# One list in place of ranks: the order of 2667 pieces of work in a sparse attention and SwiGLU kernel

## The chip, the cores and the metric

The kernel runs on one core of a Trainium2 chip. The metric is the device time of one execution in microseconds (us). Lower is better. The work is issued on five queues, each in order: TensorE (PE), VectorE (DVE), ScalarE (ACT), GpSimd (POOL), and SyncE (SP), which here only starts DMA transfers.

## The reference

Attention over 4 batches, 8 heads, 768 tokens of head size 64, with a block mask (blocks of 32 tokens: neighbours, first and last block, and 3 drawn blocks for each block row), then a SwiGLU feed-forward layer over all 3072 tokens.

```python
scores = scale * np.matmul(q, k.transpose(0, 1, 3, 2))
scores = np.where(mask, scores, -1000000000.0)
attn = np.exp(scores - max); attn = attn / (sum + 1e-09)
attn_out = np.matmul(attn, v)
x = attn_out, heads side by side            # 3072 x 512
g = x @ w_gate; val = x @ w_val             # 512 -> 1536
out = (g * sigmoid(g) * val) @ w_out        # 1536 -> 512
```

The weights arrive as 64-bit floats and are decoded on the chip.

## The kernel before

The tokens are cut into 9 chunks (`CHUNKS`): chunks 0, 1 and 2 have 256 tokens each and make up batch 0, chunks 3 to 8 have 384 tokens each. A chunk first goes through attention and then through the feed-forward layer. Chunks 0 and 1 are computed in f32, which needs only the decoded weights; later chunks use weights split into two f16 halves.

Nothing is issued where it is written. Each piece of work (a task) is handed to `add` with its engine, an estimated duration, the tasks that it needs, the ring buffers that it takes, and a rank. The tasks are numbered as they are added, 0 to 2666. `Plan.order` then plays a model of the five engines: whenever an engine is free, the ready task of the lowest rank is next on it. `SHIFT` moves the rank of groups of tasks. The order that comes out is the order of issue, and so the order in each engine's queue. Within a queue nothing overtakes: an instruction that waits holds all that stand behind it.

Names that the steps below touch:

- `load_k0` (L564, L574, L583, L581): three DMAs bring batch 0's keys as f32; PE turns six tiles (`kT`), ACT and DVE keep them (`kst`).
- `open_q0` (L1268): queries of a 128-token tile, two DMAs of 128 KB each. Chunk 0 has q0 and q1, chunk 1 q2 and q3, chunk 2 q4 and q5. Buffers: chunks 0 and 1 take ring `qs`; chunk 2 takes the ring `q`, of which there is one buffer.
- `load_v0` (L600, L609): batch 0's values in three parts of 512 KB, and four DMAs of 192 KB that spread the first and last block over the value ring.
- `pair0`: attention of two block rows of batch 0. Keys are gathered (`kring`, L1299, L1301: DVE for q0, POOL for the rest), scores (PE, L1341, L1357), `top` (DVE, L1363), `power` (ACT, L1372), `turn` (PE, L1380), `turned` (ACT or DVE, L1386), `values` (ACT or DVE, L1318), `product` (PE, L1401), `scaled` (DVE, L1409), `x_turn` (PE, L1418), a copy into `xall` (ACT, L1465).
- `norm_v0` (L398 on ACT, tile `vsq`): three squares of the values; their sum scales chunk 2 and later.
- `weights` (L453 loads, L431 to L433 decode on DVE): 12 pairs d0.0 to d0.11 for gate and value, 6 for the output. A pair takes two of four buffers of `stage`, so at most two pairs are on their way. `square_w` (L398 on ACT, tile `wsq`) and `norm_w1` follow.
- `ffn_in` (L1687 for chunks 0 and 1, L1693 later), `ffn_out` (L1756): the feed-forward matmuls, tiles `p` and `po`.
- `open_q` (L814): the norm of a later batch's queries, four DMAs of 128 KB into ring `q`; called g6 for batch 1.

In the kernel before, `behind=first_loads[-1]` chained the loads of `load_k0`, `load_v0` and `open_q0` one behind the other, so their order among themselves was fixed as they were added; weight loads came behind the seventh of them.

Of the kernel before, what the change touches and what calls it, by code (L numbers as in the profile page):

```python
# [18 lines left out]
BLK = 32  # L19
# [27 lines left out]
SHIFT = {  # L47
# [54 lines left out]
}  # L102


class Task:
    __slots__ = ("eng", "us", "emit", "need", "rank", "take", "dma", "left", "outs", "next", "ready", "end", "no", "key", "late", "many")


class Buf:


    def __init__(self, ring):
        self.ring, self.users, self.tile = ring, [], None

    def free_at(self):
        ends = [t.end for t in self.users]
        return None if None in ends else max(ends)


class Plan:  # L120


    def __init__(self):
        self.tasks, self.depth, self.given = [], {}, {}
        self.key = ""

# [3 lines left out]
    def add(self, eng, us, emit, need=(), rank=0.0, take=(), use=(), dma=None, behind=None, late=0.0, many=1):  # L130
# [14 lines left out]
        self.tasks.append(t)  # L145
        return t

    def may_take(self, t, now):

        at = now  # L150
        asked = {}
# [1703 lines left out]
```

## Time and profile before

| | |
|---|---|
| median of 3 runs | 797.4 us (796.4, 797.4, 800.65) |
| profiled execution | span 798.2 us; the page gives no other time for it |
| instructions | 21196 |
| PE busy | 762.4 us (96%) |
| DVE busy | 547.4 us (69%) |
| ACT busy | 504.5 us (63%) |
| POOL busy | 205.7 us (26%) |
| HBM read, written | 79.50 MB, 11.01 MB |

The span runs from the first to the last instruction. A busy PE is not PE at its peak: the ends of matmuls are modelled, and the clock granted to TensorE has two levels, 1.2 and 2.4 GHz; a mean of 0.67 in a stretch says that the engine ran a good part of it at the lower one. A wait names what came last before the waiting instruction began; "issue" is time in which nothing that the profile shows was waited for.

### The profile page before, as it was taken

What the parts mean: (1) busy time and instruction counts of PE and PEld (TensorE: products, weight loads), DVE (VectorE), ACT (ScalarE), POOL (GpSimd) and SP (SyncE); (2) the same over time, 40 slices, a digit from 0 to 9 for tenths busy, and PEclk for the clock granted to TensorE, in tenths of its full rate; (3) what the DMA queues carried; (4) which work ended last, traced back from release to release, by engine and by line L of the source; (5) the groups of instructions that cost most, each with busy time, mean ns of one, the idle gap of its engine ahead of it and who ended that gap; (6) DMA issues with size and microseconds to landing.
All of it is one profiled execution on the core that took longest, in us unless ns stands there. A gap on an engine that the chain in (4) does not pass through costs nothing.

```text
span 798.2 us, 21196 instructions
## 1 busy us (share of the span) xinstructions
PE 762.4 (96%) x8098; PEld 489.2 (61%) x8098; DVE 547.4 (69%) x1658; ACT 504.5 (63%) x1211; POOL 205.7 (26%) x257
## 2 busy tenths in 40 slices
PE   3789999999999999999999999999999999999998
PEld 2557778884587566645665566645665566555655
DVE  5676898998898787742799866753798767731220
ACT  2687767587688686763598856754487757641221
POOL 3553511322033223201223222401223233101210
PEclk9889999999999999999999999999999999999999
DMA  8963537647877979478769994947878974330001
GB/s 205 259 220 118 193 146 260 205 125 230 198 151 172 212 169 197 91 197 265 159 134 182 269 227 114 203 97 211 188 133 179 228 177 105 69 69 19 1 1 39
DMA packets 171430, 128.08 MB, mean 160 GB/s; under 512 B 115008, under 2 KB 136896, under 8 KB 171328
## 3 DMA queue, kind: packets, MB, share of 16 engines
q1 hardware_dynamic: 165696, 109.42, 56.6%
q0 software_dynamic: 5632, 17.31, 8.5%
q8 instruction: 63, 1.03, 0.5%
q14 instruction: 39, 0.32, 0.1%
HBM read 79.50 MB, written 11.01 MB: 113 GB/s over the span
## 4 chain that ended last, share of the span: by engine, by line
PE 63%; DVE 18%; DMA 8%; issue 4%; ACT 4%; SPq 1%; DVEq 1%; ACTq 0%
PE p L1693 29%; PE po L1756 18%; PE pv L1206 4%; PE p L1687 3%; DMA q<-in_q_dram 3%; PE qk L1137 3%; DVE pp L394 2%; DVE act L1702 1%; DVE act L1707 1%; DMA pts<-pp 1%; DVE w1t L394 1%; DVE e L1151 1%; DMA stage<-in_k_dram 1%; DVE kring L1114 1%; PE qk L1341 1%
## 5 line engine op out<-in xcount | busy, mean ns | idle before, releaser
L1693 PE MATMUL p<-xall,w1t 128*128 128x384 f16 (+1 forms) x2016 | 326.8, 319 | 0.0
L1693 PEld LDWEIGHTS <-w1t 128*128 128x128 f16 x2016 | 191.2, 98 | 115.5 <-issue 8.5
L1715 POOL TENSOR_TENSOR h<-act,h 128x384 f16<-128x384 f32 (+1 forms) x108 | 101.6, 941 | 372.5 <-ACT h L1712 372.1
L1756 PE MATMUL po<-w2all,h 128*128 128x512 f16 (+1 forms) x900 | 195.3, 371 | 0.3 <-DVE w2all L394 0.3
L1756 PEld LDWEIGHTS <-h 128*128 128x128 f16 x900 | 84.6, 98 | 93.7 <-issue 5.6
L1712 ACT CAST h<-act 128x384 f16<-128x384 f32 (+1 forms) x108 | 50.8, 471 | 82.5 <-DVE act L1707 82.2
L1124 POOL DMA_INDIRECT w2all<-vd,vidx x66 | 62.8, 951 | 150.2 <-PE pv L1206 126.7
L1702 DVE SCALAR_TENSOR_TENSOR act<-act,p 128x384 f32<-128x384 f32 (+1 forms) x108 | 54.2, 504 | 65.2 <-ACT act L1698 64.5
L1687 PE MATMUL p<-xall,w1t 128*128 128x256 f32 x384 | 88.8, 384 | 0.4 <-DVE act L1702 0.3
L1168 ACT ACTIVATE e<-e,nb,es 128x256 f32<-128x256 f32 x132 | 78.2, 593 | 2.2
L1687 PEld LDWEIGHTS p<-xall,w1t 128*128 128x128 f32 x384 | 71.4, 192 | 12.0 <-DVE w2all L394 1.4
L1698 ACT ACTIVATE act<-p,gsc 128x384 f32<-128x384 f32 (+1 forms) x84 | 47.0, 560 | 31.2 <-PE p L1693 30.6
L1707 DVE SCALAR_TENSOR_TENSOR act<-act,hs,p 128x384 f32<-128x384 f32 (+1 forms) x84 | 49.7, 591 | 21.8 <-PE p L1693 18.8
L1206 PEld LDWEIGHTS <-w2all 128*128 128x128 f16 x1584 | 55.1, 98 | 13.9 <-issue 3.8
L394 DVE SCALAR_TENSOR_TENSOR pp<-e,rr,pp 128x256 f16<-128x256 f32 x132 | 61.2, 510 | 1.3 <-ACT pp L391 1.0
L391 ACT ACTIVATE pp<-e,rr 128x256 f16<-128x256 f32 x132 | 58.1, 496 | 3.7 <-DVE rr L782 2.5
L1206 PE MATMUL pv<-pts,w2all 128*128 128x64 f16 x1584 | 57.0, 193 | 2.8 <-DMA pts<-pp 2.8
L1151 DVE CUSTOM_DVE_ANT_1 e<-qk,msk 128x256 f32<-128x256 f32 x132 | 50.0, 417 | 2.8 <-issue 2.4
L1593 ACT ACTIVATE ot<-po,oc 128x512 f32<-128x512 f32 (+1 forms) x25 | 16.7, 667 | 42.9 <-PE po L1756 42.7
L1114 DVE COPY kring<-kst 128x256 f16 x198 | 38.9, 251 | 5.6 <-PE qk L1137 5.3
L1232 DVE TENSOR_TENSOR xall<-pv,xall 64x256 f16<-64x256 f32 x66 | 27.7, 420 | 21.1 <-ACT xall L1227 18.7
L1137 PE MATMUL qk<-kring,qs 128*32 128x256 f16 x1056 | 35.7, 274 | 0.2 <-DVE mx L1151 0.2
(187 smaller groups left out, 899.4 us busy)
## 6 DMA issues: line engine op xcount, KB each, us to landing
stage<-in_w_dram SPq DMA_DIRECT2D x36, 512.0 KB
w2all<-vd SPq DMA_DIRECT2D x66, 192.0 KB
qs<-qraw SPq DMA_DIRECT2D x72, 128.0 KB
out_dram<-ot SPq DMA_DIRECT2D x19, 256.0 KB
qn<-in_q_dram SPq DMA_DIRECT2D x36, 128.0 KB
qraw<-in_q_dram SPq DMA_DIRECT2D x36, 128.0 KB
stage<-in_v_dram SPq DMA_DIRECT2D x9, 512.0 KB
vd<-stage SPq DMA_DIRECT2D x9, 512.0 KB
```

Of the source, the lines that this page charges most:

```text
L391: nc.scalar.activation(hi, src, AF.Copy, scale=scale)
L394: nc.vector.scalar_tensor_tensor(lo, src, scale, hi, op0=ALU.mult, op1=ALU.subtract)
L1124: nc.gpsimd.indirect_dma_start(vf[0:96, 1, :], None, bt.vd, bass.IndirectOffsetOnAxis(ap=vidx[0:96, qb : qb + 1], axis=0))
L1137: nc.tensor.matmul(stv[u * BLK : (u + 1) * BLK, g].rearrange("p s k -> p (s k)"), o.q[:, l, h // 2, h % 2, col : col + BLK], kg[:, h].rear ...
L1151: nc.vector.tensor_tensor_reduce(ev[:, g], stv[:, g], o.g.msk[:, qb, :].unsqueeze(2).broadcast_to([P, 8, BLK]), scale=1.0, scalar=-3.0e38, ...
L1168: nc.scalar.activation(ev[:, g], ev[:, g], AF.Exp, bias=nb_[:, g : g + 1], scale=o.g.es[:, 0:1], accum_out=c["rs"][:, g : g + 1],)
L1206: nc.tensor.matmul(pvv[:, j, n % 2], vg[:, cc, l, 2 * j : 2 * j + 2, :], pq[:, g, m, cc, u : u + 2, :], start=i == 0, stop=i == 5,)
L1687: nc.tensor.matmul(t[:, 0:tc_], w[:, i + 1, k_ * P : (k_ + 1) * P], x_k(k_), start=k_ == 0, stop=k_ == NKT - 1)
L1693: nc.tensor.matmul(t[:, 0:tc_], w_[:, f, m, k_, :], x_k(k_, l), start=i == 0, stop=i == 11)
L1702: nc.vector.scalar_tensor_tensor(a_, a_, 1.0, pg.tile[:, 0:tc_], op0=ALU.add, op1=ALU.mult)
L1715: nc.gpsimd.tensor_tensor(hv(f)[:, 1, :], act.tile[:, 0:tc_], hv(f)[:, 0, :], op=ALU.subtract)
L1756: nc.tensor.matmul(po.tile[:, cs], hv(f)[:, l, ts_], w2h[:, f, m, cs], start=f == 0 and i == 0, stop=f == NF - 1 and i == 2)
```

## The change

`SHIFT` is gone, and so are the model of the engines in `Plan.order`, `may_take` and `free_at`. `TURN` lists all 2667 task numbers; `Plan.order` walks it and only asserts that each task's needs and buffers are met. The tasks, what they issue and their needs are unchanged, except that the chain `first_loads` is gone: the loads of `load_k0` and `load_v0` have no predecessor any more, the second tile of each `open_q0` comes behind its first, and a weight pair's first load has no predecessor.

```diff
-SHIFT = {
-    "a0.0": 215.65, "a0.1": -2208.54, "a1.0": 2743.2, "a1.1": -905.98, "a2.0": -5449.96, "a2.1": 1137, "a3.0": -2069.74,
...
+TURN = [
+    7, 0, 18, 1, 2, 3, 37, 5, 8, 9, 19, 10, 20, 4, 6, 22, 12, 14, 15, 11, 13, 16, 17, 21, 42, 43, 44, 25, 83, 41,
+    39, 23, 63, 64, 65, 80, 57, 27, 26, 45, 46, 66, 67, 47, 24, 35, 49, 48, 53, 62, 40, 51, 60, 79, 81, 68, 70, 84,
...
     def order(self):
...
+        assert sorted(TURN) == list(range(len(self.tasks)))
         done = []
...
+        for n in TURN:
+            t = self.tasks[n]
+            assert not t.left, f"task {n} stands before one that it needs"
...
-        a = add("SP", 0.37, lambda: load(0), need, rank, take=raw, behind=first_loads[6], dma=1.7)
+        a = add("SP", 0.37, lambda: load(0), need, rank, take=raw, dma=1.7)
...
-            o.done = add("SP", 1.2, lambda sub=sub, si=si: load(sub, si), [], rank + 0.2 * sub, behind=first_loads[-1],
-                         take=[] if sub else [buf], use=[buf] if sub else [], dma=2.0, many=2)
-            first_loads.append(o.done)
+            o.done = opener = add("SP", 1.2, lambda sub=sub, si=si: load(sub, si), [], rank + 0.2 * sub, behind=opener,
+                                  take=[] if sub else [buf], use=[buf] if sub else [], dma=2.0, many=2)
```

With the tasks numbered as they are added, the list gives each queue its new order. The head of SP's queue (k.2 is the third part of the keys, v.0 the first part of the values, e the four spread loads, d0.0a and d0.0b the two loads of a weight pair):

```
place   before  after        place   before  after
0       table   k.2          10      d0.1a   e
1       k.0     table        11      q1      q2
2       k.1     k.0          12      v.1     v.1
3       k.2     k.1          13      v.2     d0.0a
4       q0      v.0          14      d0.1b   d0.0b
5       v.0     q0           15      d0.0a   d0.1a
6       e       e            16      d0.0b   d0.1b
7       e       e            17      q2      q3
8       e       q1           18      q3      g6, first 4 DMAs
9       e       e            19      q4      d0.2a
```

After that v.2 stands at place 23 (before 13), the loads of d0.4 at 24 and 25 (before 25 and 26), q4 at 26 (before 19), q5 at 33 (before 22); from place 54 to 62 the two orders agree.

On the other queues, counted in tasks: the values copies w0.0 and w0.1 on DVE move from places 12 to 14 to places 18, 20 and 22, behind the first four `top`. On ACT the three value squares leave places 8, 15 and 17 for places past 60, and the weight squares q1.0 leave places 28 and 29 for 39 and 36. The decode of d0.1 moves on DVE from 28 to 30 to 44, 45 and 48. On PE the first feed-forward piece moves from place 37 to 31, chunk 2's first scores stay at 53. In chunks 3 to 8 the 45 score pieces move on PE by between 3 places later and 15 earlier, 5.5 earlier in the mean; the 78 products by between 7 later and 9 earlier, 1.0 earlier in the mean. For one pair of chunk 6 (b6.1.0 and b6.1.1) scores move from 341 to 326, the first product from 349 to 343. The norms of later values and keys (v1, k1, v2, k2, v3, k3) come 2 to 11 PE places earlier. The last 38 PE pieces (from the second piece of chunk 8's feed-forward layer on) stand as before.

## Rows read from the trace of the kernel before

**Rows 1.** Windows: stretch, length; PE, PEld, DVE, ACT, POOL busy; clock, DMA share, GB/s
```profile
0.00:10.00 10.00, 2.31 (x11) 2.28 (x12) 4.23 (x25) 1.88 (x2) 2.62 (x9) 1.00 0.66 196
10.00:20.00 10.00, 5.14 (x82) 3.17 (x81) 7.31 (x24) 3.92 (x6) 3.92 (x4) 0.88 1.08 214
20.00:30.00 10.00, 7.25 (x146) 5.30 (x145) 5.29 (x15) 6.29 (x22) 3.08 (x13) 0.67 1.05 306
30.00:60.00 30.00, 23.43 (x632) 15.97 (x631) 21.41 (x47) 23.18 (x61) 19.41 (x37) 0.90 0.77 218
60.00:100.00 40.00, 37.53 (x599) 30.55 (x598) 30.90 (x73) 29.22 (x75) 17.09 (x26) 0.98 0.47 156
100.00:160.00 60.00, 59.56 (x573) 48.73 (x572) 56.98 (x114) 39.34 (x97) 13.06 (x12) 1.00 0.60 202
160.00:200.00 40.00, 37.31 (x174) 24.96 (x173) 34.49 (x84) 33.58 (x62) 10.03 (x10) 1.00 0.59 176
200.00:600.00 400.00, 394.86 (x4112) 243.12 (x4111) 290.97 (x983) 274.31 (x667) 96.26 (x105) 1.00 0.79 179
```

**Rows 2.** Waits of PE over the whole span: total us, times, longest us
```profile
PE qk L1341 <- DMA q<-in_q_dram: 3.1, 2, 2.6
PE pv L1206 <- DMA pts<-pp: 2.8, 3, 1.3
PE pt L1380 <- ACT e L1372: 2.6, 4, 1.2
...
PE nrm_v L388 <- ACT stage L398: 2.4, 2, 1.3
```

**Rows 3.** Chain of work, first 40 us: start us, us, what
```profile
3.46 9.84 DMA q<-in_q_dram
13.31 13.91 DMA q<-in_q_dram
```

**Rows 4.** Timeline of SP's queue: start us, us, what, count
```profile
2.72 1.60 SPq L1268 DMA_DIRECT2D q<-in_q_dram  x2
4.36 0.88 SPq L600 DMA_DIRECT2D w2all<-in_v_dram  x1
5.28 4.30 SPq L609 DMA_DIRECT2D w2all<-in_v_dram  x4
...
12.24 1.61 SPq L1268 DMA_DIRECT2D q<-in_q_dram  x2
...
55.43 0.81 SPq L453 DMA_DIRECT2D stage<-in_w_dram  x2
```

**Rows 5.** Timeline of PE: start us, us, what, in brackets the idle time before
```profile
13.34 0.39 PE L1341 MATMUL qk<-kst,q 64*32 64x96 f32 x14 [0.47 <-DMA q<-in_q_dram]
...
18.47 0.32 PE L1357 MATMUL qk<-dupm,ones_h 128*128 128x192 bf16 x1 [0.96 <-issue]
...
26.90 0.77 PE L1341 MATMUL qk<-kst,q 64*32 64x96 f32 x9 [2.61 <-DMA q<-in_q_dram]
```

**Rows 6.** Timeline of DVE, values copies, first top, decode of d0.1
```profile
17.24 2.89 DVE L1318 COPY w2all<-w2all 32x512 f32<-32x512 f32 x6 [1.28 <-issue]
...
20.79 1.28 DVE L1363 TENSOR_REDUCE mx<-qk 128x2 f32<-128x512 f32 x2
...
34.99 0.68 DVE L431 TENSOR_SCALAR w1t<-stage 128x1024 int32<-128x1024 int32 x1
...
36.97 1.23 DVE L433 SCALAR_TENSOR_TENSOR w1t<-stage,w1t 128x1024 int32<-128x1024 int32 x1
```

**Rows 7.** Timeline of ACT, one value square and one weight square
```profile
30.97 1.05 ACT L398 ACTIVATE vsq<-w2all 128x1024 bf16<-128x1024 f32 x1
...
43.86 1.06 ACT L398 ACTIVATE wsq<-w1t 128x1024 bf16<-128x1024 f32 x1 [0.47 <-DVE w1t L433]
```

**Rows 8.** Timeline of PE, first feed-forward piece, chunk 2's first scores
```profile
60.50 1.71 PE L1687 MATMUL p<-xall,w1t 128*128 128x256 f32 x4
...
68.80 0.40 PE L1341 MATMUL qk<-kst,q 64*32 64x96 f32 x16
```

More of the change, by code (lines that the diff above doesn't have):

```diff
@@ L44 @@
 LANES = 8
-SHIFT = {
[54 rows of a table removed]
-}
+TURN = [
[137 rows of a table added]
+]
 class Task:
@@ L113, in __init__ @@
         self.ring, self.users, self.tile = ring, [], None
-    def free_at(self):
-        ends = [t.end for t in self.users]
-        return None if None in ends else max(ends)
 class Plan:
@@ L134, in add @@
         t.key = self.key if rank > -50.0 else ""
-        t.rank = rank + SHIFT.get(t.key, 0.0)
+        t.rank = rank
         t.need = [x for x in need if x is not None]
@@ L146, in add @@
         return t
-    def may_take(self, t, now):
-        at = now
-        asked = {}
-        for b in t.take:
-            n = asked.get(b.ring, 0)
-            asked[b.ring] = n + 1
-            i = len(self.given[b.ring]) + n - self.depth[b.ring]
-            if i >= 0:
-                given = self.given[b.ring]
-                f = given[i].free_at() if i < len(given) else None
-                if f is None:
-                    return None
-                at = max(at, f + SEM_US)
-        return at
@@ L164, in order @@
-    def order(self):
-        free = {}
-        waiting = {}
-        for t in self.tasks:
-            free.setdefault(t.eng, 0.0)
-            waiting.setdefault(t.eng, [])
-            if not t.left:
-                waiting[t.eng].append(t)
-        queue = 2.0
-        lanes = [0.0] * LANES
-        done = []
-        now = 0.0
-        while len(done) < len(self.tasks):
-            later = []
-            moved = False
-            for eng, list_ in waiting.items():
-                if free[eng] > now:
-                    later.append(free[eng])
-                    continue
-                best = None
-                for t in list_:
-                    if t.ready > now:
-                        later.append(t.ready)
-                        continue
-                    if best is not None and (t.rank, t.no) > (best.rank, best.no):
-                        continue
-                    at = self.may_take(t, now)
-                    if at is None:
-                        continue
-                    if t.many:
-                        at = max(at, lanes[t.many - 1])
-                    if at > now:
-                        later.append(at)
-                        continue
-                    best = t
-                if best is None:
-                    continue
-                t = best
-                list_.remove(t)
-                for b in t.take:
-                    self.given[b.ring].append(b)
-                free[eng] = now + t.us
-                t.end = now + t.us + t.late
-                if t.dma is not None:
-                    queue = max(max(queue, now + min(0.4, t.us)) + t.dma, t.end)
-                    t.end = queue + DMA_US
-                    for _ in range(t.many):
-                        lanes.append(max(lanes.pop(0), t.end))
-                for x in t.outs + t.next:
-                    x.ready = max(x.ready, t.end + SEM_US if x in t.outs else free[eng])
-                    x.left -= 1
-                    if not x.left:
-                        waiting[x.eng].append(x)
-                t.ready = now
-                done.append(t)
-                moved = True
-                later.append(free[eng])
-            if not moved:
-                assert later, "the tasks wait for one another"
-                now = min(x for x in later if x > now)
@@ new lines, in order @@
+    def order(self):
+        assert sorted(TURN) == list(range(len(self.tasks)))
+        done = []
+        for n in TURN:
+            t = self.tasks[n]
+            assert not t.left, f"task {n} stands before one that it needs"
+            for b in t.take:
+                b.taken = True
+                i = len(self.given[b.ring]) - self.depth[b.ring]
+                assert i < 0 or None not in [u.end for u in self.given[b.ring][i].users], f"task {n} takes a buffer in use"
+                self.given[b.ring].append(b)
+            t.end = float(len(done))
+            for x in t.outs + t.next:
+                x.left -= 1
+            done.append(t)
@@ L301, in tile_block_sparse_attn_swiglu @@
     tab = const.tile([P, NB * 6], I32, name="tab")
-    first_loads = []
-    def first(load):
-        first_loads.append(load)
-        return load
     def load_tab():
@@ L369, in tile_block_sparse_attn_swiglu @@
     t_pre = add("DVE", 1.5, before, [], rank=-250.0)
-    t_tab = add("DVE", 0.75, tables, [first(add("SP", 0.4, load_tab, rank=-400.0, dma=0.4, late=1.2)), t_pre], rank=-200.0)
+    t_tab = add("DVE", 0.75, tables, [add("SP", 0.4, load_tab, rank=-400.0, dma=0.4, late=1.2), t_pre], rank=-200.0)
     t_rep = add("DVE", 2.0, repeats, [t_tab], rank=TAB)
@@ L565, in load_k0 @@
                 raw[:, 2 * i : 2 * i + 2, :], k[0, i * 256 : (i + 1) * 256, :].rearrange("(t p) n -> p t n", p=P)),
-                [], rank, behind=first_loads[-1], dma=1.7))
-            first(loads[-1])
+                [], rank, dma=1.7))
         for t in range(NTB):
@@ L599, in part @@
         def part(i, rank):
-            bt.v0_loads.append(first(add("SP", 0.45, lambda i=i: nc.sync.dma_start(
+            bt.v0_loads.append(add("SP", 0.45, lambda i=i: nc.sync.dma_start(
                 v0[:, 2 * i : 2 * i + 2, :], v[0, i * 256 : (i + 1) * 256, :].rearrange("(t p) n -> p t n", p=P)),
-                [], rank, behind=first_loads[-1], dma=2.0)))
+                [], rank, dma=2.0))
         bt.v0_part = part
@@ L608, in load_v0 @@
             for n, r0 in enumerate((0, S - BLK)):
-                e0_done.append(first(add("SP", 0.45, lambda m=m, sl=sl, n=n, r0=r0: nc.sync.dma_start(
+                e0_done.append(add("SP", 0.45, lambda m=m, sl=sl, n=n, r0=r0: nc.sync.dma_start(
                     w2all[sl, n + 2 * m : 2 * V0_RING : 4, :],
-                    v[0, r0 : r0 + BLK, :].unsqueeze(1).broadcast_to([BLK, V0_RING // 2, DM])), [], rank, behind=first_loads[-1], dma=0.8)))
+                    v[0, r0 : r0 + BLK, :].unsqueeze(1).broadcast_to([BLK, V0_RING // 2, DM])), [], rank, dma=0.8))
     def more_v0(rank):
@@ L1257, in open_q0 @@
         o = Tile_q()
-        view = {}
+        view, opener = {}, None
         def load(sub, si):
```

188 rows, old and new, of tables (SHIFT, TURN) are left out of this document.

## The prediction

> **What bounds the kernel now.** I read the page's engine shares first: PE is busy for 762.4 of 798.2 us, so what an order can win is at most the 35.8 us in which PE is idle, and what its clock loses. The second view, the busy times by stretch, shows where that is [rows 1]. PE is idle for 7.7 us in the first ten, 4.9 in the next ten, 2.8 from 20 to 30, 6.6 from 30 to 60, 2.5 from 60 to 100, 0.4 from 100 to 160, 2.7 from 160 to 200, and 5.1 over the 400 us after that; what is left, 2 to 3 us, lies after 600, in the tail. So the kernel is bound by PE from about 60 us on, and by a mixture before. The reader should also see there that the clock was granted at 0.88, 0.67 and 0.90 of full speed from 10 to 60 us: busy time times the missing share is 5.14 x 0.12 + 7.25 x 0.33 + 23.43 x 0.10 = 5.4 us of PE work lost. And DVE is busy for 57.0 of 60 us from 100 to 160: there it is nearly as tight as PE.
>
> The third view, PE's waits, names causes: query loads 3.1 us, transposed probabilities in later chunks 2.8, the exponentials of batch 0 2.6, norms of values 2.4 [rows 2]. The fourth, the chain of waits in the first 40 us, consists of two query loads, 9.8 and 13.9 us long [rows 3]. The fifth, the queues' own timelines, says what each of these stood behind [rows 4 to 7].
>
> **The change part by part.** No instruction is added or removed, so every term is idle time or clock. Against the profiled execution, 798.2 us; the median of the runs is 797.4, and I take off 0.8 at the end.
>
> *Start and first queries.* The keys are loaded first as before, another part ahead; three parts and the table are the same bytes, so I count nothing, though after the last part PE has three tiles to turn instead of two. But q0 now stands behind the values' first part. Before, q0 was issued at 2.72, before the values' 0.88 us of issue [rows 4], and landed at 13.31 [rows 3]. Issued 0.9 later it lands at 14.2 at best. At worst it waits until both it and the values are in: the values copies on DVE begin at 17.24 [rows 6]. I take the middle, 15.7.
>
> The scores of the first pair started at 13.34 and the first `top` at 20.79 [rows 5, 6]. Between lie matmuls, which I estimate at 3.2 us (PE was busy for 5.14 us from 10 to 20, which holds the end of the turned keys too [rows 1]), and several waits, one of them 0.96 us of "issue" [rows 5] that I can't assign. With q0 at 15.7, 3.2 us of work and half a microsecond of such waits, `top` starts at 19.5, since no 2.89 us of values copies stand ahead of it on DVE any more [rows 6]. Gain 1.3. Bounds: 3.6 gained with q0 at 14.2 and no wait, 1.5 lost with q0 at 17.2 and all of the waits.
>
> The Trainium skill bears on this step ("DMA: Bandwidth & Descriptors", Queues, rings and completion order): each engine takes the descriptors of a ring in ring order. [...]
>
> *Second queries.* q1 was issued at 12.24, after all four spread loads (4.30 us of issue) and a weight load, and landed at 27.22 [rows 3, 4]; PE stood for 2.61 us until 26.90 [rows 5]. Now only two of the spread loads stand before it. Its issue follows from the issue times [rows 4]: 2.72, when table and keys are issued, + 0.88 values + 1.60 q0 + 2.15 for two spread loads = 7.35. With q0's 9.8 to 10.6 us from issue to landing it is there at about 17.9, with q1's own 15.0 at 22.3. PE was free for these scores at 26.90 - 2.61 = 24.3 and now is at 24.3 - 1.3 = 23.0, so the whole 2.61 us goes. Bounds: 0 (landing as late as before) and 2.61. What is late next is `kring` on POOL, which from 60 us backwards is the least loaded engine [rows 1].
>
> *What leaves the heads of ACT and DVE.* Three value squares of 1.05 us and two weight squares of 1.06 leave ACT's early queue [rows 7]: 5.3 us that stood between exponentials. The decode of d0.1, from 34.99 to 38.20, leaves DVE's [rows 6]: 3.2 us ahead of a `top`. PE's idle time from 30 to 60 us is 6.6 [rows 1], of which 2.6 are waits for exponentials [rows 2]. These pieces don't vanish; they are done later, where ACT has room (39 of 60 us busy from 100 to 160) but DVE has little (57.0 of 60). So I take a bit under half, 3.0. Bounds: 0 (all of it comes back) and 6.6.
>
> *Clock.* From 20 to 30 us 2.4 of the 5.4 us are lost, in the stretch with q1's stall. PE was idle there for 2.61 us before 26.90 [rows 5]. Without it I give back half, 1.2. Bounds 0 and 4.
>
> *Values' third part, q4, q5, g6.* v.2 comes ten places later on SP. Its first reader is then a value square past place 60 on ACT, so nothing waits unless the loads of d0.2 and d0.3 ahead of it hang on slow decodes. q4 goes from place 19 to 26, behind g6's first loads, and both need the single `q` buffer. Cost nothing if q4 lands before chunk 2's scores, which started at 68.80 [rows 8]; the place before it (d0.4's second load) was reached at 55.43 [rows 4]. This is the second rival below.
>
> *Later chunks.* Idle PE time from 160 to 600 us is 7.8 [rows 1], of which 2.8 are waits for transposed probabilities [rows 2]. Scores come 5.5 places earlier in the mean and products 1.0, so a product has 4 to 5 PE pieces more between it and its scores: that should shorten those waits. Against it, six norms come 2 to 11 places earlier and may stand longer for their squares (2.4 us before, for values). I take 0. Bounds: 2.8 gained, and 4 lost. The tail is the same 38 pieces: 0.
>
> Sum: 1.3 + 2.6 + 3.0 + 1.2 = 8.1; 798.2 - 8.1 - 0.8 = **789.3 us**. All good bounds together, 3.6 + 2.6 + 6.6 + 4 + 2.8 = 19.6, give 777.8; all bad ones, -1.5 - 4 = -5.5, give 802.9.
>
> **The rivals.**
>
> *The gain is given back (no change).* Early attention ends sooner, but the feed-forward layer of chunks 0 and 1 needs decoded weights, and DVE, which decodes them, is at 57.0 of 60 us from 100 to 160 [rows 1]. If the deferred 3.2 us of d0.1 and the rest of DVE's queue don't move forward into its idle time (22 us idle before 60, 9 from 60 to 100 [rows 1]), PE waits there for what it saved. For it: that tightness. Against it: the idle DVE time is just where the change puts attention earlier. Then only the 1.2 us of clock and a little remain: about 796.
>
> *Chunk 2's queries come too late (slower).* q4 waits for the `q` buffer until the square of g6's first load is done, 47 places down ACT's queue, and SP holds d0.6, d0.5, d0.7 and q5 behind it. If q4 is issued only at 55.4 + 0.8 = 56.2, where the place before it was done [rows 4], and takes the 15.0 us that q1 took, it lands at 71.2. PE, 8 us ahead, is at these scores at 60.7 and stands for 10.5 with everything behind it; the weights held back on SP cost as much again as one decode, 3.2. That gives 798.2 - 8.1 + 10.5 + 3.2 - 0.8 = 803.0. The point from which it decides is a landing of q4 later than about 61. For it: both orders of buffers and the late place. Against it: DMA engines are only 0.47 busy from 60 to 100 against 1.05 at the time of q1 [rows 1], so the landing should be much quicker.
>
> *The early stage fills completely (faster than forecast).* PE gets attention pieces without a break from 16 us on, the clock stays up, the whole of 6.6 and 4 come, and the later waits go: near 780. For it: DVE was idle for 22 of the first 60 us. Against it: products still need gathers on POOL and copies on ACT, 23.2 of 30 us busy from 30 to 60 [rows 1].
>
> **How the numbers follow.** Forecast (784 to 793) 0.56; given back (793.5 to 798) 0.17; q4 late 0.10; filled (776 to 784) 0.17. A difference of 0.5%, 4.0 us, is about what a measurement of this kernel can tell from no change. Faster than 793.4 takes the forecast and the filled case, 0.73; slower than 801.4 takes most of the late case, 0.08, and 0.02 for waits in the later chunks, 0.10; the rest is 0.17. The range is 778 to 798: below it lies little of the filled case, above it the late case and a tail of the given-back one. The forecast's own range is 784 to 793.
>
> **What would show each step.** In the new profile q0 should land at 14 to 17 us and q1 before 23, with no wait of PE for queries over 1 us. The first `top` should begin before 20. Value and weight squares should lie behind the exponentials of chunks 0 and 1, the first feed-forward matmul on PE should begin before 55 instead of at 60.50 [rows 8], and PE's idle time from 10 to 60 should fall from 14.2 to about 7. PE's waits for `pts` should not exceed 2.8 us, for norms not 6. Wrong would be: a wait of several us at chunk 2's scores on `q`, new idle PE time from 60 to 160 with DVE's decode as releaser, or waits spread over chunks 3 to 8.

## The result, and the profile after

The changed kernel takes 805.9 us, the kernel before 800.6 (medians of 13 runs each, side by side). The ratio, which leaves out one run of the kernel before that took 883.5 us, is 1.0077 [1.0052, 1.0102]: slower by 0.5 to 1.0%, where 789.3 us and a gain of 1% were forecast, and outside the range of 778 to 798. The profiled execution has a span of 805.2 us against 798.2, so 7.0 us are to be found.

The windows of the kernel after, in the same stretches and columns as [rows 1]:

```profile
0.00:10.00 10.00, 2.27 (x10) 1.90 (x11) 2.82 (x17) 1.31 (x2) 0.62 (x7) 1.00 0.60 202
10.00:20.00 10.00, 6.37 (x80) 4.41 (x78) 6.32 (x30) 2.27 (x4) 5.69 (x6) 0.85 1.12 209
20.00:30.00 10.00, 8.05 (x251) 6.02 (x246) 6.55 (x14) 6.76 (x23) 4.30 (x15) 0.81 1.05 312
30.00:60.00 30.00, 21.89 (x565) 16.35 (x547) 17.78 (x35) 18.70 (x55) 16.38 (x31) 0.89 0.59 145
60.00:100.00 40.00, 34.80 (x583) 27.49 (x581) 33.34 (x80) 33.34 (x79) 18.92 (x26) 0.96 0.61 193
100.00:160.00 60.00, 58.21 (x566) 47.88 (x565) 55.81 (x101) 38.20 (x94) 13.81 (x15) 1.00 0.64 211
160.00:200.00 40.00, 37.43 (x174) 25.49 (x174) 34.25 (x89) 34.39 (x65) 10.28 (x11) 1.00 0.59 162
200.00:600.00 400.00, 393.05 (x4157) 243.55 (x4156) 301.58 (x1018) 281.07 (x687) 94.74 (x103) 1.00 0.79 180
```

PE is idle for 3.6 us from 10 to 20 (4.9 before) and 2.0 from 20 to 30 (2.8), as hoped. Then it turns: 8.1 from 30 to 60 (6.6), 5.2 from 60 to 100 (2.5), 1.8 from 100 to 160 (0.4), 7.0 from 200 to 600 (5.1). From 10 to 60 us it sums to 13.7, where 14.2 were to become about 7. The columns after PEld say more: DVE does 33.5 us of work in the first 60 us (2.82 + 6.32 + 6.55 + 17.78), where it did 38.2, and ACT 29.0 against 35.3. That work is still to be done.

PE's waits, the lines that answer to [rows 2] and the new ones (total us, times, longest):

```profile
PE qk L1352 <- issue: 10.4, 7, 5.5
PE pv L1412 <- DMA w2all<-in_v_dram,vidx: 2.7, 1, 2.7
PE qk L1149 <- DVE mx L1163: 2.6, 3, 1.5
PE qk L1352 <- POOL kring L1312: 1.6, 1, 1.6
PE p L1704 <- DVE act L1713: 1.3, 1, 1.3
```

The wait for query loads (3.1 us) is gone from the list. In its place stands "issue", 10.4 us at the scores of batch 0. From the timeline of PE, the scores of q0 (two, then the other fourteen), the longest such wait, and the first feed-forward piece (start, us, what, in brackets the idle time before):

```profile
13.38 0.39 PE L1352 MATMUL qk<-kst,q 64*32 64x96 f32 x2
13.98 0.39 PE L1352 MATMUL qk<-kst,q 64*32 64x96 f32 x14 [0.21 <-issue]
...
36.03 0.79 PE L1352 MATMUL qk<-kring,q 64*32 64x160 f32 x15 [5.49 <-issue]
...
53.94 1.24 PE L1698 MATMUL p<-xall,w1t 128*128 128x256 f32 x5
```

The first feed-forward piece comes at 53.9 instead of 60.5 [rows 8], but six PE pieces fewer stand ahead of it (place 31 instead of 37), so this is not a lead of 6.6 us. To see what was won and where it went, compare starts at places of PE's queue that hold the same piece in both orders, with the same set of pieces before it. Place 60 is a feed-forward piece of chunk 0, place 74 one of chunk 1, place 154 the first of chunk 2, place 209 the second one of chunk 3. Of the kernel before:

```profile
86.84 1.89 PE L1687 MATMUL p<-xall,w1t 128*128 128x256 f32 x8
...
104.11 1.99 PE L1687 MATMUL p<-xall,w1t 128*128 128x256 f32 x8 [0.30 <-DVE act L1702]
...
215.23 0.94 PE L1693 MATMUL p<-xall,w1t 128*128 128x256 f16 x7
...
284.85 1.47 PE L1693 MATMUL p<-xall,w1t 128*128 128x384 f16 x8
```

And of the kernel after (the piece of place 209 lies inside the last group and starts at 290.5):

```profile
84.29 1.97 PE L1698 MATMUL p<-xall,w1t 128*128 128x256 f32 x8
...
104.42 1.89 PE L1698 MATMUL p<-xall,w1t 128*128 128x256 f32 x8
...
216.99 1.26 PE L1704 MATMUL p<-xall,w1t 128*128 128x256 f16 x10
...
289.50 2.11 PE L1704 MATMUL p<-xall,w1t 128*128 128x384 f16 x12
```

So PE is 2.5 us ahead at place 60, 0.3 behind at place 74, 1.8 behind at place 154, 5.6 behind at place 209 (69.7 us between the last two before, 73.5 after), and 6.7 at the last matmul (794.7 and 801.4). Nearly all of the loss lies ahead of place 209. Each of these is one execution, and executions differ: with the same order up to place 154 as the kernel before, e2, e6 and e10 come to it at 212.8 to 213.2 instead of 215.2. The time from place 154 to 209 repeats better: 69.6 to 70.5 us in the five kernels of this document that keep the order before in this stretch (before, e4, e6, e12, e14), 72.6 to 73.5 in the eleven with the new order on both sides of place 154 and all of its work (after, e3, e5, e7 to e9, e11, e13, e15 to e17). Between the two places, from the windows, first before, then after:

```profile
215.20:284.90 69.70, 68.13 (x949) 51.36 (x946) 58.46 (x238) 54.72 (x155) 20.64 (x25) 1.00 0.78 174
```

```profile
217.00:290.50 73.50, 69.00 (x946) 51.91 (x945) 65.76 (x242) 59.27 (x163) 20.72 (x25) 1.00 0.84 176
```

DVE has 65.8 us of work there instead of 58.5, and PE is idle for 4.5 us instead of 1.6. The groups of instructions on DVE in those stretches show which (count, total us, mean ns), before and after:

```profile
L394 DVE SCALAR_TENSOR_TENSOR w1t<-w1t,wsc 128x512 f16<-128x512 f32 x1 | 0.7, 744 | 0.0
```

```profile
L407 DVE SCALAR_TENSOR_TENSOR w1t<-w1t,wsc 128x512 f16<-128x512 f32 x7 | 5.2, 745 | 0.0
```

These are low halves of the split of the gate and value weights into f16. The new list puts seven of them behind place 154, between the `top` pieces of chunk 3 (DVE places 284 to 341, chunk 3's first `top` at 265). In the order before all 24 stand ahead of chunk 3's first `top`; one of them was still done after 215.2.

### The profile page after: what moved, and what is told of

It reads as the page before. It is cut to its first block, busy times and chain, and to the rows that moved or that the text cites. A ratio compares the mean times of both kernels' runs of the same rounds, so it can differ in the third digit from the quotient of the medians.

```text
span 805.2 us, 21103 instructions
## 1 busy us (share of the span) xinstructions
PE 761.7 (95%) x8098; PEld 490.9 (61%) x8098; DVE 553.8 (69%) x1658; ACT 503.8 (63%) x1211; POOL 205.3 (26%) x257
## 4 chain that ended last, share of the span: by engine, by line
PE 67%; DVE 13%; issue 6%; DMA 6%; ACT 5%; POOL 1%; SPq 1%; DVEq 1%; POOLq 0%; ACTq 0%
PE p L1704 31%; PE po L1767 22%; PE pv L1218 4%; PE qk L1149 3%; DMA stage<-in_w_dram 2%; PE qk L1352 2%; PE p L1698 1%; PE qkf L934 1%; DVE kring L1126 1%; DVE pp L407 1%; DMA w2all<-in_v_dram,vidx 1%; DVE act L1718 1%; PE pvf L1003 1%; DVE act L1713 1%; DVE e L1163 1%
## 5 line engine op out<-in xcount | busy, mean ns | idle before, releaser
L1726 POOL TENSOR_TENSOR h<-act,h 128x384 f16<-128x384 f32 (+1 forms) x108 | 97.1, 904 | 408.7 <-ACT h L1723 376.4
L1767 PE MATMUL po<-w2all,h 128*128 128x512 f16 (+1 forms) x900 | 191.4, 371 | 1.4 <-DVE act L1713 0.8
L1767 PEld LDWEIGHTS <-h 128*128 128x128 f16 x900 | 86.4, 98 | 95.7 <-issue 3.2
L407 DVE SCALAR_TENSOR_TENSOR pp<-e,rr,pp 128x256 f16<-128x256 f32 x132 | 63.1, 522 | 7.0 <-ACT pp L404 4.8
L1218 PEld LDWEIGHTS <-w2all 128*128 128x128 f16 x1584 | 52.6, 98 | 11.0 <-issue 3.5
L1604 ACT ACTIVATE ot<-po,oc 128x512 f32<-128x512 f32 (+1 forms) x25 | 16.6, 666 | 37.3 <-PE po L1767 32.2
```

The costliest lines, as they stand in the source:

```text
L407: nc.vector.scalar_tensor_tensor(lo, src, scale, hi, op0=ALU.mult, op1=ALU.subtract)
L1218: nc.tensor.matmul(pvv[:, j, n % 2], vg[:, cc, l, 2 * j : 2 * j + 2, :], pq[:, g, m, cc, u : u + 2, :], start=i == 0, stop=i == 5,)
L1726: nc.gpsimd.tensor_tensor(hv(f)[:, 1, :], act.tile[:, 0:tc_], hv(f)[:, 0, :], op=ALU.subtract)
L1767: nc.tensor.matmul(po.tile[:, cs], hv(f)[:, l, ts_], w2h[:, f, m, cs], start=f == 0 and i == 0, stop=f == NF - 1 and i == 2)
```

## The experiments

Two theories came out of the traces. F: PE's "issue" waits are instruction fetch held up by data. During each of the two long ones a 16 KB transfer of the queue that section 3 of the page calls instruction is on its way, and they begin after PE's instructions 449 and 705, 256 apart (weight loads and all else in its queue counted). G: work for DVE was put off and comes back where DVE is nearly full.

**Which part costs: the early order, the late order, or the form?**

```diff
 e1: -TURN = new order
     +TURN = new order up to PE place 154, then the order before
 e2: -TURN = new order
     +TURN = order before up to PE place 154, then the new order
 e6: -TURN = new order
     +TURN = order before (as a list, without the chain of first loads)
```

> The new order for everything up to the 154th PE piece (about the first 195 us), then the rest in the order of before. PE's idle time up to 200 us was 27.5 us before and 31.0 after, beyond it 8.3 and 12.5. Theory S (two separate losses): this kernel keeps the early 3.5 us and gives up the late 4.2, so about 801 to 802 us of span, a ratio to before of 1.004. Rival L (the late loss follows from the early one, because what is late at 200 us stays late): ratio near 1.008. Rival M (all of it is the late part): 1.000.

Measured 1.0134 [1.0093, 1.0174], more than any of the three theories said. The cut itself makes a wait, so this run does not price the early order. It moves the last low halves ahead of chunk 3's first `top`, nine in a row, each of which waits for its high half on ACT; PE stands for 7.3 us, and takes 80.5 us from place 154 to 209. PE's wait, and one of the nine:

```profile
PE qk L1157 <- DVE mx L1171: 7.3, 1, 7.3
```

```profile
208.20 0.75 DVE L415 SCALAR_TENSOR_TENSOR w1t<-w1t,wsc 128x512 f16<-128x512 f32 x1 [0.72 <-ACT w1t L412]
```

> The order of before up to the 154th PE piece, then the rest in the new order. Theory S: the late 4.2 us alone, ratio 1.005, PE idle before 200 us as before (27.5 us), beyond it near 12. Rival L: 1.000, the late order costs nothing once the early part is in time. Rival M: 1.008.

Measured 0.9971 [0.9945, 0.9998]. The late order as a whole does not cost. In this run all 24 low halves stand ahead of chunk 3's first `top`, as before, and the rest is the new order from place 154 on; place 209 comes 71.5 us later:

```profile
212.80:284.28 71.48, 68.50 (x948) 51.78 (x945) 62.66 (x246) 56.30 (x159) 22.42 (x25) 1.00 0.81 169
```

> The order of before, written as a list in the new kernel, with the chain of first loads gone. If the order alone counts: ratio 1.000 within 0.3%, the same waits as before. Rival: the form or the chain costs something, ratio off 1 by more than 0.5%.

Measured 1.0001 [0.9976, 1.0025]. The list and the missing chain cost nothing. With e2, the loss is in the order up to about place 154 on PE and in what it puts off past that place.

**Theory F: early waits**

```diff
 e3: -raw[.., n*512 : (n+1)*512] as four pieces of 512 bytes a row (open_q)
     +raw[sl, n*512 : (n+1)*512] from 512 neighbours, one piece of 2 KB a row
 e4:  order before, SP:  -q3, q4, ...   +q3, g6 first 4 DMAs, ..., q4
 e5:  the new kernel again, on another chip
 e7:  new order, SP:  -d0.0a d0.0b d0.1a d0.1b q3 g6
                      +q3, 16 bytes written once the 2nd pair's rr is there, d0.0a d0.0b d0.1a d0.1b g6
 e8:  new order, POOL: -key copies of b2.0.0, its two value gathers
                       +its two value gathers, key copies
 e9:  e3 + e7 + e8, and the next pair's gathers early too
```

> The new order unchanged; the queries that are loaded for a batch's norm alone (open_q) come in pieces of 2 KB instead of 512 bytes, the same bytes in another arrangement, which leaves the sum of squares as it is. Theory F (PE waits for its instructions, whose 16 KB fetch stands among the 512-byte pieces of the norm load on the DMA engines): the wait of 5.5 us at 30.5 us, in the middle of a score piece, falls below 2 us and the span by 3 to 5 us, to about 801. Rival W (the fetch takes its time whatever the other transfers are, or the wait has another cause): the wait stays between 4.5 and 6.5 us and the time at the new kernel's, ratio 1.008.

Measured 1.0034 [1.0004, 1.0064]. The wait that was to fall below 2 us is 3.84 (and the one ahead of it 2.65). e18 has 3.84 there too, with the short pieces: no support for the piece size.

> The order of before, with one thing of the new one: the first norm load of batch 1's queries (four DMAs in 512-byte pieces) goes to place 19 of SP's queue, its square to ACT's place 51, and chunk 2's first queries come behind. Theory F: a wait of PE on issue alone, 2 to 5 us long, appears between 28 and 42 us, and the time is 2 to 4 us longer, ratio 1.003 to 1.005. Rival W: no new wait of that kind, ratio 1.000, or a loss only at chunk 2's first scores, at about 69 us.

Measured 0.9999 [0.9971, 1.0027]. A wait appears where F puts it, behind instruction 705, and the time does not move. e14, which does not load the norm early, has one of 2.0 us at the same instruction, so the norm load is not shown to be its cause:

```profile
30.75 0.38 PE L1360 MATMUL qk<-kst,q 64*32 64x96 f32 x3 [2.41 <-issue]
```

> The new kernel itself, on the chip that runs the next three. All theories: ratio to before 1.005 to 1.010. Theory F (PE waits for its instructions): PE stands on issue exactly behind its 449th and its 705th instruction, 256 apart, each time for a 16 KB fetch that runs late, 6 to 7.5 us together, and chunk 2's feed-forward layer begins at 208 to 217 us as in the two profiles of this early order so far. Rival N (what the first profile showed was that one run's): the waits stand elsewhere or are under 3 us together.

Measured 1.0059 [1.0036, 1.0083], with waits of 1.2 and 6.0 us at the same two instructions.

> The new order, but the first four weight loads (2 MB) and the norm load stand behind q3 and behind a 16-byte transfer that waits for the second pair's reciprocals (34 us in the last profile, sooner if PE isn't held up); the first decode pass comes three DVE places later. Theory F: with those 2.5 MB out of the way the fetches that PE needs behind its 449th and 705th instruction run 1 to 3 us after they are asked for instead of 5 to 6; the two waits fall from 6.5 to under 3 us together, the first feed-forward piece begins 3 to 5 us sooner than in the new order on this chip, and the time falls by 2 to 5 us unless the later weights cost it: ratio 1.001 to 1.005. Rival W (a fetch takes 6 us whatever else is on its way): the waits stay at 6 to 7 us, the weights come later, ratio 1.008 to 1.012.

Measured 1.0051 [1.0024, 1.0077]. The timeline of PE, at the same two instructions:

```profile
27.50 0.49 PE L1364 MATMUL qk<-kring,q 64*32 64x160 f32 x12 [1.28 <-issue]
...
31.25 0.50 PE L1364 MATMUL qk<-kring,q 64*32 64x160 f32 x15 [1.10 <-issue]
```

The two waits fall from 7.2 (e5, same chip) to 2.4 us, which supports F on what they are. The time falls by 0.1%, within the error, but the price of the waits is not isolated by that: 2 MB of weights come later here, and new waits of the kind appear, of 1.1 and 1.5 us behind instructions 961 and 1217. All of PE's "issue" waits from 20 to 217 us come to 9.5 us in e5 and still to 8.5 in e7.

> The new order, with the two gathers of chunk 2's first pair (POOL) ahead of that pair's key copies, as they stood before, instead of behind four more key copies. Theory G (PE's wait of 2.7 us for gathered values, with 1.6 us for POOL's key copies in front of it, is a loss of its own): the 2.7 us go and the time falls by 2 to 3 us against the new order on this chip, ratio 1.004 to 1.006. Rival D (behind it PE would have waited for decoded weights or chunk 2's chain anyway): the wait goes, others take its place between 85 and 160 us, ratio as the new order's, 1.007 to 1.009.

Measured 1.0038 [1.0017, 1.0058]. The wait of 2.5 us near 91 is gone, and the next pair's gathers make one of 3.2 us:

```profile
104.42 1.08 PE L1420 MATMUL pv<-w2all,pts 128*32 128x64 f32 x32 [3.23 <-DMA w2all<-in_v_dram,vidx]
```

> The new order with three repairs at once: the first four weight loads and the norm load of batch 1 held behind q3 and a 16-byte marker transfer, the norm loads in pieces of 2 KB (other elements of the queries are squared, the sum is the same), and the gathers of the next two pairs ahead of the key copies on POOL. Alone they gave about 0.1%, 0.3 to 0.4% and 0.1 to 0.2%. If the loss of the new order is made of these early waits, they add up to some 0.6%: ratio 0.999 to 1.002 against the kernel before. If each repair only moves the wait to the next place (rival), the ratio stays at 1.003 to 1.006.

Measured 1.0062 [1.0039, 1.0085]. PE now reaches place 154 at 212.8, level with e10 on the same chip (212.9), yet takes 73.1 us to place 209, and the ratio is that of the new order (one execution of each; that of e9 is the fastest of its eleven). Where the early waits were, PE now waits for DVE, 4.2 us where it was 1.7 in the kernel after:

```profile
PE pv L1444 <- DVE xs L1435: 4.2, 3, 3.5
```

Taking the early waits away does not bring the loss back.

> The kernel before's order up to PE piece 154, then the new order (0.997 by itself), and the norm loads in pieces of 2 KB. If long pieces help because the transfers of all four batches' norms take less of the DMA engines whatever the order, the ratio is 0.993 to 0.996. If they only helped the new early order (the instruction fetch behind g6's first loads), it stays at 0.996 to 0.998.

Measured 0.9998 [0.9971, 1.0026] (e2's order with e3's loads; 71.6 us from place 154 to 209). Long pieces bring nothing there, so what e3 seemed to gain is not shown to be theirs.

**Loads or computing pieces?**

```diff
 e11: new order,    SP places 0 to 53:  -new   +as before
 e12: order before, SP places 0 to 53:  -as before   +new
```

> The new order, but the first 54 places of SP's queue as in the kernel before (the other queues follow the new order except where a piece must wait for its load: 10 places on PE, 21 on DVE, 85 on ACT shift). If the loss of 0.6 to 0.8% comes from the order of the loads, the ratio falls to 0.998 to 1.001. If it comes from the order of the computing pieces (rival), it stays at 1.004 to 1.008. In between, both have a share.

> The mirror image: the kernel before's order, with the first 54 places of SP's queue as in the new order (some places between 26 and 43 can't follow because of the buffers; 59 places on PE, 106 on DVE, 74 on ACT shift). If the order of the loads costs, the ratio is 1.003 to 1.008; if the order of the computing pieces costs, 0.998 to 1.001. The forecast's own term for the loads (second queries early, 2.6 us, and the clock, 1.2 us) would make it 0.995.

Measured 1.0307 [1.0271, 1.0343] and 1.0809 [1.0772, 1.0845], far outside all that was expected. Crossing one queue with four others makes waits that neither kernel has. Of e11, then of e12:

```profile
PE nrm_w L409 <- ACT wsq L419: 7.1, 2, 6.8
```

```profile
PE pv L1420 <- ACT pts L1405: 17.1, 5, 12.3
PE pv L1437 <- DVE xs L1428: 11.9, 6, 5.4
```

They tell nothing on the question, except that queues of one list are tuned to each other.

**Theory G: work put off on DVE**

```diff
 e13: new order, DVE:    decode of d0.0 to place 29, behind the eighth top, that of d0.1 to 37
 e14: order before, DVE: decodes of d0.0, d0.1, d0.3 as late among the attention pieces as in the new order
 e15: e13, and d0.2, d0.3, d0.4 two to seven places earlier
 e16: new order, DVE:    decode of d0.0 at places 26 to 28, ahead of the top that waits for PE until 37.4 us
 e17: e16, SP:           -g6, d0.2a, d0.2b   +d0.2a, d0.2b, g6
 e18: new order, split_w, last five gate and value pairs:
-        return add("DVE", 0.67, lambda: lo_part(lo, src, scale, hi), [t1], rank)
+        return add("DVE", 0.67, lambda: nc.gpsimd.memset(lo, 0.0), [t1], rank)
```

> The new order with one change, on DVE alone: the decode of d0.0 stands behind the sixth top (before the wait that ends at 37.1 us) instead of at places 35 to 43, that of d0.1 three pieces later instead of 44 to 48. Theory G, deferred decode: in the new order no weights are loaded from 39 to 51.6 us, since both pairs' buffers wait for these decodes, DVE does 5 us less by 60 us than in the kernel before and is nearly full from 100 to 220, so the f16 split of the weights is 5 us behind at chunk 2 and chunk 3 pays again. Then the next loads start before 45 instead of at 51.6, and the ratio falls from 1.006 to 1.008 to 0.998 to 1.002. Theory F, instruction fetch behind saturated DMA engines: nothing changes there, 1.004 to 1.008.

> As the one with d0.0 and d0.1 decoded early, and the decodes of d0.2, d0.3 and d0.4 two to seven places earlier on DVE as well. Theory G: at least as good as that one, 0.995 to 1.001, since the loads of the following pairs move up too. Rival: the tops behind these decodes come late and PE waits for exponentials between 40 and 60 us, then 1.002 to 1.006 with new waits of PE for e.

Measured 1.0141 [1.0104, 1.0179] and 1.0150 [1.0102, 1.0198]: both worse, and by my own reading error. The edit put the decode behind the eighth `top`, not the sixth, and the timeline of DVE in e13 shows that the seventh is the one that waits for PE (the decode begins two pieces behind it):

```profile
37.44 0.69 DVE L1382 TENSOR_REDUCE mx<-qk 128x2 f32<-128x512 f32 x1 [5.29 <-PE qk L1376]
...
39.73 0.69 DVE L452 TENSOR_SCALAR w1t<-stage 128x1024 int32<-128x1024 int32 x1
```

So 6 us of decode stood between exponentials, and in e13 PE waited for transposed probabilities (3.0 us) and scaled values (3.6 us).

> The mirror image: the kernel before's order, with the decodes of d0.0, d0.1 and d0.3 as late among the attention pieces on DVE as in the new order (d0.0 and d0.1 behind the tops of the sixth pair, d0.3 behind d0.2; 41 of 877 pieces on DVE, 15 on ACT and 5 on PE shift). Theory G: 3 to 6 us lost, ratio 1.004 to 1.008, and more f16 splits behind chunk 2's first feed-forward piece than in the kernel before. Theory F: no change, 0.998 to 1.002.

Measured 1.0170 [1.0132, 1.0208], worse than G's 1.008. Part of it is another wait than in the new kernel, since PE's queue has the weights' norm early:

```profile
52.92 0.16 PE L409 MATMUL nrm_w<-wacc,ones_h 128*128 128x2 bf16 x1 [7.26 <-ACT wsq L419]
```

That wait is most of what e14 loses by place 154 (221.8, against 213.2 in e6). That putting decodes off costs is shown for this order; its size in the new kernel is not. From place 154 to 209 e14 takes 70.5 us, as the order before does, so late decodes alone do not lengthen that stretch.

> The new order with the decode of d0.0 alone (three pieces, 3.1 us) moved on DVE from places 35 to 43 to place 26, ahead of the top that waits for PE until 37.4 us: into a stretch in which DVE is idle. (e13 had put it behind that top, so it did not use the idle time.) Theory G, deferred decode: the loads of d0.2 start at 36 instead of 51.6, DVE has 3 us of its backlog done in idle time, ratio 1.001 to 1.005 against 1.006 to 1.008 of the new order. If the backlog on DVE is not the cause: 1.005 to 1.009.

Measured 1.0035 [1.0013, 1.0056]. The four loads of d0.2 and d0.3 begin at 32.6 instead of 51.6 (timeline of SP below; the last ends at 51.1, since d0.1 is decoded as late as in the new order), and PE comes to place 154 at 209.6, against 212.2 in e18 on the same chip, which has the new order's decodes:

```profile
32.61 18.47 SPq L474 DMA_DIRECT2D stage<-in_w_dram  x4
```

With three us of decode in DVE's idle time PE is 2.6 us earlier at place 154 (e17, with the same decode: 209.6 as well; one execution of each); from there to place 209 it takes 73.0 us still.

> As e16, and on SP the norm load of batch 1 behind the loads of d0.2, so that its 512-byte pieces fall into the stretch from 39 to 51 us in which the DMA engines are empty. Theories F and G together: the instruction fetch after PE instruction 705 comes sooner, its wait of 6 us falls below 3, and the ratio is 0.997 to 1.003. If the early waits are made up later whatever they are (as e9 suggests): as e16.

Measured 1.0025 [1.0005, 1.0046]. Not told apart from e16; the wait after instruction 705 is 3.8 us (2.7 in e16), where it was expected below 3.

> The new order, with the low halves of the last five pairs of gate and value weights (ten pieces of 0.75 us on DVE, of which seven come after the first feed-forward piece of chunk 2) left out: GpSimd sets them to zero instead. It leaves out part of the computation. Theory G, DVE is what is late around chunk 2 and 3: PE pieces 154 to 209, 73.4 us in the new order and 70 in the kernel before, take 70 to 71.5 us; ratio 1.001 to 1.005. If DVE's backlog does not hold PE there: 73 us and 1.005 to 1.008. Risk: the zeroing on GpSimd delays the gathers behind it.

Measured 0.9994 [0.9977, 1.0012]. The stretch from place 154 to 209, in the windows:

```profile
212.20:281.50 69.30, 67.81 (x946) 51.67 (x945) 59.56 (x232) 58.64 (x163) 24.18 (x32) 1.00 0.93 187
```

With these ten low halves off DVE (the zeroing on GpSimd takes 0.55 us each), DVE has 59.6 us of work there and PE takes 69.3 us, as in the kernel before (69.7) and 4.2 less than in the kernel after; stretch and ratio are both better than expected. PE is idle for 1.5 us of it, where it was 4.5. So DVE's work holds PE up in this stretch.

But e18 leaves the pieces out, which says more than what their place costs. e2 and e10 have the new order from place 154 on, with all 24 low halves done ahead of chunk 3's first `top`, and take 71.5 and 71.6 us. By these, of the 3.8 us some 2 go with the place of the seven halves, and the other 1.8 stay when they are ahead, with 62.7 us of work on DVE instead of 58.5. (These two also differ from the kernel after in the order ahead of place 154.) The kernel before without these low halves was not run; PE is idle there for 1.6 us of the 69.7, so it could not win much more than that. The new order with the seven pieces spread ahead of place 154, and that together with e16, were not tried either, and e1 shows that a row of them right ahead of the `top` costs PE 7.3 us. That another place for them would bring the new order below the kernel before is only argued.

## Why the prediction was wrong

*Start and first queries (1.3 gained).* The first `top` began at 20.45 instead of 20.79: 0.3 gained. The first two of q0's scores began at 13.38 (at 12.52 before, ahead of the row that I showed), and the weight loads of the other fourteen waited 0.43 us for q0, until 13.97, sooner than the 14.2 that I called best:

```profile
13.97 0.18 PEld L1352 LDWEIGHTS qk<-kst,q 64*32 64x32 f32 x14 [0.43 <-DMA q<-in_q_dram]
```

But waits of "issue" of 1.17 and 1.10 us between 16.6 and 19.2 took the rest, the very kind of wait that I had said I could not assign. My bad bound, 17.2 for the values, did not come either: ACT copies their first part at 13.88.

```profile
13.88 0.61 ACT L1329 COPY w2all<-w2all 96x512 f32<-96x512 f32 x1
```

The rule that descriptors of a ring are taken in ring order (the Trainium skill, "DMA: Bandwidth & Descriptors", Queues, rings and completion order) agrees with that as far as it goes: the first part of the values, issued ahead of q0, was in by 13.88, all of q0 by 13.97.

*Second queries (2.6 gained).* Right as a wait: no wait of PE for queries is left. Much of it was given back at once, in the "issue" wait of 5.5 us that ends at 36.03.

*Clock (1.2 gained).* The granted clock was 0.85, 0.81 and 0.89 from 10 to 60: 6.37 x 0.15 + 8.05 x 0.19 + 21.89 x 0.11 = 4.9 us lost against 5.4, so 0.5 gained.

*What leaves the heads of ACT and DVE (3.0 gained, bounds 0 and 6.6).* This is the step that failed, in sign. I wrote that the pieces are done later, where DVE has little room, and then priced that at no worse than zero, without a reason for the floor. A DVE that was busy for 57 of 60 us did not take work later for nothing. The loads of the next pairs also wait for the stage buffers that these decodes free: SP's queue in the kernel after shows it,

```profile
25.19 6.21 SPq L826 DMA_DIRECT2D qn<-in_q_dram  x4
51.61 4.98 SPq L466 DMA_DIRECT2D stage<-in_w_dram  x4
```

and from 39 to 51 us the DMA engines are busy to a share of 0.19, where it was 0.84. At place 60 PE is 2.5 us ahead, about what the other three terms gave (0.3 + 2.6 + 0.5 = 3.4); at place 154 it is 1.8 behind. So 4.3 us went on the way, in this pair of executions, where 3.0 were to be gained. e16 supports that a part of that is the decode. The waits that one sees there, fetch and gathers, are not worth their length: where e7, e8 and e9 shorten them, others take their place, in e9 waits for DVE.

*Later chunks (0, bounds 2.8 gained and 4 lost).* Wrong by 3.8 us, between places 154 and 209. That is inside the bad bound by luck, since the bound was for norms that wait for their squares, and no such wait stands in this stretch. I followed loads, decodes, squares, scores and products through the two orders, but not the split pieces `lo_part`, seven of which the list moves behind chunk 3's first `top`. Without them the 3.8 us are gone (e18); with them ahead about half is (e2, e10). Beyond place 209 the term was right: 509.8 us to the last matmul before, 510.9 after (515.3 in e6, which has the order before), and e2 at 0.997.

*The rivals.* "The gain is given back" named the right engine and a mechanism close to the one seen, at 0.17, but I ended it at "no change". The slower rival, chunk 2's queries late, did not happen: no wait for them is in the list. The range stopped at 798 since I gave only 0.10 to any loss.

*Settled and open.* The form and the chain cost nothing (e6), and the late order as a whole costs nothing (e2). Of a loss of 5 to 6 us in the medians (e5 and the kernel after), 2 to 4 lie between places 154 and 209 in every execution; there DVE's work holds PE up (e18), and some 2 us of that go with the place of the seven low halves (e2, e10). What keeps the other part of that stretch is not shown. The rest, 1 to 4 us, is ahead of place 154 or within what executions differ by; that it is DVE work put off is supported by e16 and by the direction of e14, not shown. What the fetch waits cost is open, since e7 moved them more than it removed them. The ratio of the unchanged new order on the chip of e16 to e18 was not measured (1.006 and 1.008 on two others), so these shares are good to about a quarter of a per cent.

## What to carry to other kernels

When pieces move later, follow every one of them to the place where it now stands and ask which engine is full there; "all of it comes back" is not a floor of zero here but hid a cost, since that engine was the tight one. Compare two orders at places where the same work has been done, not at clock times or at the first piece of a kind: that left 2.5 us of a seeming early gain of 6.6, and showed the loss behind it. Leaving work out shows which engine is late; what a place in the order costs needs a run that only moves the work. And a visible wait is worth its length only if nothing else is late right behind it; shortening three of them here (e9) brought nothing.

## What the hardware did that I had not expected

PE seems to have run out of instructions. Section 3 of the page of the kernel after shows the queue that brings them:

```profile
q8 instruction: 63, 1.03, 0.5%
```

63 transfers of 16 KB. PE stands after its instructions 449 and 705, 256 apart, and such a transfer starts at 25.2 and 33.0 us, 2.7 and 3.0 us before PE goes on, while the DMA engines are busy with data to a share of 1.05: for 1.6 and 5.5 us in the kernel after, for 1.3 and 1.1 when the weight loads are held back and the share from 20 to 32 us is 0.53 (e7). In e7 the next such waits, 1.1 and 1.5 us, come behind instructions 961 and 1217, again 256 apart. The trace names "issue", since PE waits for nothing that it shows. In the window from 34 to 36 us no engine works at all:

```profile
34.00:36.00 2.00, 0.00 (x0) 0.00 (x0) 0.00 (x0) 0.00 (x0) 0.00 (x0) 0.50 1.09 162
```

On this reading, loads that fill the DMA engines early slow the engine that they are meant to feed, by waits that no data dependence explains. What such a wait costs the whole kernel is not shown here.
